# Two convolutions and a joint network on one core: a leading tile of 360 outputs, triple tiles of 214 and 334, and conv1's weight sums spread over PSUM and GpSimd

## The chip, the core and the metric

The kernel runs on one core of one Trainium2 chip. The metric is the device time of one execution in microseconds. Five engines work side by side, each through its own queue in order, and wait for one another on semaphores: TensorE (PE; its weight loads are listed as PEld), VectorE (DVE), ScalarE (ACT), GpSimd (POOL), and SyncE (SP), whose queue issues nearly all DMA transfers here.

## The reference

```python
B, T, D, K, U = 2, 4000, 512, 5, 8
xp = pad(x, 2)                                    # along time
h = gelu(sum_i xp[:, i:i+T] @ w1[i])[:, ::2]      # conv1, every second output: 2000
f = gelu(sum_i hp[:, i:i+T1] @ w2[i])[:, ::2]     # conv2 of padded h, again every second: 1000
fe = f @ w_f;  ge = g @ w_g
j  = tanh(fe[:, :, None, :] + ge[:, None, :, :])  # 2 x 1000 x 8 x 512
out = j @ w_o
```

Inputs, weights and the output are bfloat16.

## The kernel before

Channels lie on the 128 partitions in four blocks (`NK` = 4); time runs along the free dimension. conv1 of the first sequence is done in three tiles, conv1 of the second in two, conv2 in one a sequence.

**The leading tile** (`direct`, L691) is a plain convolution: the first 408 outputs (`2 * NA`, `NA` = 204), five taps by four output blocks `m` by four input blocks `k`, 80 matmuls of 408 columns that accumulate in PSUM banks 0 to 3. Its input `xr` comes in by two plain DMAs (128 rows of four time steps, then the rest), is turned by TensorE (`turn`, L489: 32 transposes, 16 of them 128 columns wide and 16 of the rest's 78) and copied out of PSUM to `xs` by ScalarE and VectorE. Eight warming matmuls of 512 columns on a cleared tile `zero` (L419, `warm_mm`, L480) come before.

**The triple tiles** (`Triple`, L562, and `Unit`, L607) use a fast form that makes three neighbouring outputs from nine products instead of fifteen. A tile of n columns gives 3 n outputs; for each output block `m` (a unit) it issues nine products of four matmuls: t2, tm, sm, t1, s1, t0, s0, ti, si, of n columns each. The two tiles of the first sequence are 266 columns each (`N3`), their six input phases are read by transposing DMAs into `xq[0]` and `xq[1]` (`load_xq`, phases in the order 4, 0, 2, 1, 3, 5). Before its products a tile needs differences and sums of its input phases in `row` (`Triple.step`: d2, d1, d0 are doubled copies on ScalarE, the others are differences or sums on VectorE), and the products need combinations of the weights: `w1_x[0..2]` for tm, t2, sm and `w1_t[0..2]` for s1, s0, t1. These are made once by `w1part` (L542), in four pieces of 128 columns: a piece has five VectorE operations of 512 elements with fp32 intermediate results in SBUF (t = w0 + w4, u = 4 w4 + w0, u = 2 w2 + u, v = t - w2, t + w2) and two copies on ScalarE; the first and the third piece also make the combinations of w1[1] and w1[3] for two pieces.

Then come conv2 in two triple tiles of 334 columns, the features, and the joint: 31 groups of seven products (`Seven`), a form that saves one of eight half-size products, with sums on GpSimd or VectorE, evicting copies on ScalarE or VectorE, and stores.

**The order** of each engine's queue is written out by hand as a string of two-character numbers (`ORDER`, L69): the operation's place in the program's text. `Plan.edges` (L148) derives which operation depends on which from the cells of SBUF and the PSUM banks that they touch, and `emit` (L211) puts a semaphore wait where the two are on different engines. Operations made with `flex` may run on one of two engines; the string that lists them decides. The durations written at the operations (`cost`, `wire`) do not enter the program. Since every queue is in order, an operation that waits holds up all that stands behind it on its engine.

**Loads.** SP issues `xr` in two parts, then w1[0] in halves, w1[4] in halves, w1[2], w1[1], w1[3], each held back until an earlier one has landed (`gate`), then xq[0], xq[1] and `xp[2]`, six phases each. GpSimd clears the few columns behind the data of xq[1] once its phases have landed (L678). xq[0] shares its place with xs[1], xq[1] with the end of `w2_sb`.

Of the kernel before, what the change touches and what calls it, by code (L numbers as in the profile page):

```python
# [7 lines left out]
ACT = mybir.ActivationFunctionType  # L8
ALU = mybir.AluOpType
# [54 lines left out]
class Op:  # L64
# [6 lines left out]
        "0Y0Z0a0b0c0d0e0f0g0i0k0l0n0q0y0z0_0-101112131415161718191A1B1C1D1E1F1G1H1p2L2l321I1J2v2S2T1r1s2w2n2N2o2O34352y2V2z2W"  # L71
        "3F3G3C3D392s3X2t3A3Y3Q3S3g3T403a3b3q4A3n3i3r3j3d4J423e4T4B434U3o473t4L4j4M4D3u484E4h4W4Q4k4R5U4X4u4r4x4s4o524z4p4_4v"
        "5e55565y535f586667595W5X5b5c6U5_6W5h6e6X5-6f6u6h6i6364695i6-726b6c6w6A736x707H7a7J7K7y7R7k7O7l7S7h7U7P757V7i7c867d7_"
        "7-767n8c8C897o8A8M87838N8J848e8K8f8E8F8v8_8w8m8n989990918j8P958k8Q9B8x8y9M9O8p9P8q9T9U969Z9a9c9C9o9x9d9W9z9X9qA5ACA2"
        "ABA4A99sAWAGAI9tArAsANAKB3B4BAAiAQAjATBBARAUBMAlAmBeBNAoApBfBtAyAzBGBhBiA-BTBUB0BDBHBEBJCABzBaBKBbBWBXCBBkBlCQCHB_CI"
        "CNBnC0COC1BqBoCKBrCLCuCcC6CdCRCfCvCgCTCjCkC7CxCyCUDODSDBDCDTC_DeDEC-DFCnCoD1DVD2DWDfDYDKDZDlDoDLDpDmDwE1E2D4E4E5D5Db"
        "DcDxDsDtENE7E8EOEKEDEEEiEAEjEBELEcEXEYEdF7ETEoFLEUF0EfElFMEgF1F8FXEmFDFOFfF3FBFPFgFsF4F_G4F-FRFiG5FZFjFSFUFVG1G2GNGG"
        "GHGTGUFoFpFuGAGWG7G8GZGXGJGKGOGaGnGoGcGqGrGhGfHCGwGxH0GdHEH3H1HVH4H9HWHAHbHhH6I4I5HKHNHcHLH7HOHjHpHqHeHYHZHfHRHSIAI7"
        "I8IKHyHzHsIhIbIBILHtIcIiIDJ4J5INIOIRIeISIEIkJKIrIsIfJAJBIlJLJDI_J7IuIvJXI-J8JdJaJbJYJEJgJeJRJNJhK0K1JnJoJSJqJwJOKGK6"
        "JrK3K4KHKbJxK7KVKWK9KcKAKYKZL0KeKfKlKmKNL1KOKJKuL6KKKoL7LZKpL3LTL9KvLGLULaLHLALcL4LyLNLsLjLOLkLtLzLdLJLKLWM2LXM3MCMR"  # L80
        "L-M0MSMuMDMvLmLnM5MJM6MhMiMKMFMUMXMGMVMYMaMxMyMbM_N1M-NPN8N9MoMkNQMpN2MlNBNCNFNGNSNTNYNuNvO1ONNZOONfNgNiNjNVNWN_O2Nx"
        "NyN-O8OdNmOeNnO9OwOTOWOUOxOqOrOXOBOQOCOtOROFOkOuOGP4OzP5OgPBPCOlOhP7O_PHPIPKP8PLPiQ9PjPQPRPNPOQAPXPYPaPrPoPpPbPsPlPm"
        "PyPePfPzQMP-Q0Q3Q4QNQCQDQIQJQFQGQPQQQTQUQXQYQbQeQfQi"),
    "act": (
        "080h0m1U0r1x1W1a1z1Z251Y2b1q271K2m1L2M1-1j2U1t2x1l1M1O332d2R1N3E2g2f2X2u2_3Z3B3H3R2h3h413c2r3K3s3M4K3x3f4C4V3p3y3w38"
        "494F4b3m3W3v4i5V5D464t4Y4P4S4y4d5C574q4w5z5B4n6E5A5g5154685d6V6g786j6v6G6M6a5j65795S6B5a745T627I7A7b6d7s5x7z7T717N6_"
        "7W7j7m5q6T7Q5w778D8d7u7g828O8B886s6t7p6S8X8-8L858o8Y9A8W9G8I8R8i8l9N7G948r9I976m9b9V9D9e9S8z9p9_9rA69YAcAXA8AFAtAdAP"
        "AfAMAeAhASAnBOAVB8BuB9AgBgCFCECs9wB7CGCqB-CJC2CCCrCDCeCwChDQCtDPDRFJDDD-CpE0DGDgEaDnFHCXEbE3D6FxFFFGFID_FwEMEFEZEPGS"
        "FyEpFNF2FYFKG_FCF5FhFzIWFkG-GIGVFvI0IVJ2GpGRGgGsHDJVH2J_HXI2IYHMHPI6I1IXIaJ-IMICIjJ6IdJ3ItI3IZJMIwJWJZK_JfK2JpKTJsNN"
        "KILSKdKRK-KnL2KUKyKqLwL8LVLILRLlL_NqKSLxM4MTMEMwMtMjMHKzMQNsN0MPMmNDNLNRMsOPNhNwNXNkNtNMOfOMNOODNrOpP6OLOiPJOoP9PPPZ"  # L90
        "PkQBPcPqP_Q1QOQHQRQgQdQk"),
    "dve": (
        "000j0o0p1R1S1v1T1V1X231w1u212Z1_1y24221b2a261d1c1Q1e1g1f1P1h1i1k28202p1m2P2Y362c1n2Q2q372e1o302i2k2j2-3U3I3V313J3L3k"
        "3P3z3l3O3N4H3-444I3_4N454Z4l4G4m4a4O4c4-4f4e504g5m5E5G5F5k5Y6D6J6F6C5l5Z5P6Y6l6L6K6Z605Q615N5O5t5p6I7C6H7D7Y6y7B5R5u"
        "6z7L7M7Z6P7q5o7X6Q5r7E6k5s5v7r7e6N806O7t7f6R816p7v6n7w6o6q7x6r8G7F8H8b8g8Z8h8u928t939H8a9F9h9f9Q9l9j9R9g8s9k9J9E9i9n"
        "9y9K9-A09mADA3A7AAA1AEAJ9uAHAOAL9vB5B69LAkAYAZBPAbAuBQAvBCAqA_BjBVBIBFBvB1BYBcBmBLByCaBpCMCPBsCZClC8CzCbCVDUCSD0CWD8"
        "DkDXEyEGEzEHD3DqDMDaE6DdDyDuEqDzEtErGCE9EkECEeEvFbEwEVEhEnFEF9FQExGjFtG6G0FTFaFWG3FqGBG9GYGLGbGPGiHHIGHlHIGyGeHFH5Hi"
        "HBHdH8HkHrHaHgHTI9H_HuIHIoJGIPIFITIgJHIpImJCJ9J0JcJFJjKDJkJiJPJTK5JyKXK8KBKaKgKPKLKjKkLDM8KwLbLfM9L5LBLPLuLYLLM1LeLo"
        "M7MAMBMdN4MLMZMWMzNAMqMcNHNUN3OZNdNbO4NcO5NaO3NzNoOAOVO0OsOSOyOvOHOmPDOYO-PMP2PTPuP3PUPvPSPnPgPtQ5QEQKQVQZQcQj"),
    "pool": (  # L100
        "01020304050s0t0u2A0v0w0x295n8VAaBSAwBRAxBwCYDjBxD9D7DhDiE-DAE_EJEsEIFcEuFeGkFdGlGDHGGFGEHmIIGmHoHJHnJIInIqIJJJKCJlKF"
        "KhKEJmLCKiLFLgLELiLhMfMeN5MgN6N7NeO6O7OaOcObP0P1PWPVPwPx"),
    "sp": (
        "0607090A0B0C0D0E0F0G0H0I0J0K0L0M0N0O0P0Q0R0S0T0U0V0W0X2B2C2D2E2F2G2H2I2J2K5H5I5J5K5L5M8S8T8UB2BZBdC3C4C5C9CiCmDHDIDJ"
        "DNDrDvEQERESEWF6FAFlFmFnFrGMGQGtGuGvGzHQHUHvHwHxH-IQIUIxIyIzJ1JQJUJtJuJvJzKMKQKrKsKtKxLMLQLpLqLrLvMIMMMNMOMnMrNENINJ"
        "NKNlNpOEOIOJOKOjOnPAPEPFPGPdPhQ2Q6Q7Q8QLQSQWQaQh"),
}


class Plan:  # L110


    COMPUTE = ("pe", "act", "dve", "pool")
    HOP = 0.16

    def __init__(self, nc):
        self.nc = nc
# [1118 lines left out]
```

## Time and profile before

| | |
|---|---|
| three runs, median | 248.95 us (248.75 to 248.99) |
| span of the profiled execution | 247.2 us |
| runs' median less that span | 1.75 us |
| PE busy | 242.8 us, 1932 matmuls |
| DVE busy | 224.8 us |
| ACT busy | 210.7 us |
| POOL busy | 83.8 us |
| granted clock of TensorE | full in all 40 slices |

The profiled execution's own time is its span, from its first instruction to its last; the times of the runs also hold what lies around it. Shares are of the span. In a row of a timeline the first number is the start, the second the length, then engine, line, operation, tiles (written <- read), shape and count; in brackets stands the idle time before it and what ended it. Most matmuls bear the line of one helper (L412), so groups are told apart by tiles and shapes. PEclk is the clock that the throttle granted; whether the array runs at full pace is read from the distance between matmuls.

### The profile page before, as it was taken

What the parts mean: (1) busy time and instruction counts of PE and PEld (TensorE: products, weight loads), DVE (VectorE), ACT (ScalarE), POOL (GpSimd) and SP (SyncE); (2) the same over time, 40 slices, a digit from 0 to 9 for tenths busy, and PEclk for the clock granted to TensorE, in tenths of its full rate; (3) what the DMA queues carried; (4) which work ended last, traced back from release to release, by engine and by line L of the source; (5) the groups of instructions that cost most, each with busy time, mean ns of one, the idle gap of its engine ahead of it and who ended that gap; (6) DMA issues with size and microseconds to landing.
All of it is one profiled execution on the core that took longest, in us unless ns stands there. A gap on an engine that the chain in (4) does not pass through costs nothing.

```text
span 247.2 us, 5277 instructions
## 1 busy us (share of the span) xinstructions
PE 242.8 (98%) x1932; PEld 186.1 (75%) x1932; DVE 224.8 (91%) x403; ACT 210.7 (85%) x359; POOL 83.8 (34%) x90
## 2 busy tenths in 40 slices
PE   8999999999999999999999999999999999999995
PEld 4657888877666666666567888778788888888883
DVE  1799998867999999699998999999999999999994
ACT  3269799899669857986799999999999999999992
POOL 1000000000000000000015584677887886796861
PEclk9999999999999999999999999999999999999999
DMA  6998999997700340000000234413433655356377
GB/s 215 331 193 168 185 157 205 150 177 174 254 2 3 119 135 3 1 1 3 0 0 3 85 102 139 143 48 129 131 127 103 195 171 172 132 187 200 123 258 233
DMA packets 57890, 31.87 MB, mean 129 GB/s; under 512 B 33835, under 2 KB 57659, under 8 KB 57865
## 3 DMA queue, kind: packets, MB, share of 16 engines
q1 hardware_dynamic: 57577, 31.41, 48.5%
q8 instruction: 15, 0.25, 0.4%
q10 hardware_dynamic: 288, 0.13, 0.2%
q14 instruction: 10, 0.08, 0.1%
HBM read 7.66 MB, written 16.38 MB: 97 GB/s over the span
## 4 chain that ended last, share of the span: by engine, by line
PE 98%; DVE 0%; issue 0%
PE acc L412 97%; PE acc L496 1%; DVE ost L835 0%; DVE xs L505 0%; DVE zero L419 0%
## 5 line engine op out<-in xcount | busy, mean ns | idle before, releaser
L398 DVE TENSOR_TENSOR og<-acc,sn 128x512 bf16<-128x512 f32 x93 | 60.0, 690 | 1.9 <-PE acc L412 1.2
L412 PE MATMUL acc<-tw,ss 128*128 128x256 f16 x372 | 58.0, 273 | 0.0
L404 ACT ACTIVATE jT<-feT,geT 128x1000 bf16<-128x1000 f32 (+6 forms) x56 | 53.2, 1002 | 1.8 <-DVE feT L398 1.5
L834 ACT ACTIVATE sn<-acc 128x512 f32<-128x512 f32 (+1 forms) x70 | 43.0, 707 | 1.0 <-PE acc L412 0.7
L412 PEld LDWEIGHTS acc<-tw,ss 128*128 128x128 f16 x372 | 36.0, 98 | 6.5 <-ACT sn L834 0.2
L903 POOL TENSOR_TENSOR ss<-jT 128x512 f16<-128x512 bf16 x24 | 27.7, 1168 | 25.0 <-DVE feT L398 22.5
L412 PE MATMUL acc<-row,w_sb 128*128 128x334 bf16 (+1 forms) x192 | 31.7, 296 | 0.0
L412 PE MATMUL acc<-wo_sb,jT 128*128 128x256 bf16 x176 | 29.2, 273 | 0.0
L404 ACT ACTIVATE sd<-acc 128x334 f32<-128x334 f32 (+1 forms) x48 | 20.6, 435 | 10.1 <-PE acc L412 9.6
L412 PE MATMUL acc<-row,w_x 128*128 128x266 bf16 (+1 forms) x192 | 28.4, 291 | 0.0
L404 ACT ACTIVATE jX<-feT,geT 128x1000 bf16<-128x1000 f32 (+4 forms) x28 | 27.4, 1042 | 0.0
L394 POOL MEMSET hT<- 128x8 bf16 (+2 forms) x6 | 0.7, 149 | 70.5 <-ACT hT L404 70.5
L412 PEld LDWEIGHTS acc<-row,w_sb 128*128 128x128 bf16 x192 | 18.7, 98 | 6.3
L412 PEld LDWEIGHTS acc<-row,w_x 128*128 128x128 bf16 x192 | 18.7, 98 | 5.7
L903 POOL TENSOR_TENSOR ss<-jT,ss 128x512 f16<-128x512 bf16 x14 | 16.6, 1189 | 15.1 <-DVE ss L903 9.7
L412 PE MATMUL acc<-wo_sb,ss 128*128 128x256 bf16 x124 | 21.0, 273 | 0.0
L412 PEld LDWEIGHTS acc<-wo_sb,jT 128*128 128x128 bf16 x176 | 17.2, 98 | 3.1
L835 DVE COPY sn<-acc 128x512 f32<-128x512 f32 (+1 forms) x25 | 16.8, 691 | 1.1 <-PE acc L412 1.0
L412 PE MATMUL acc<-hT,w_sb 128*128 128x334 bf16 x96 | 17.1, 305 | 0.0
L518 DVE SCALAR_TENSOR_TENSOR acc<-acc,sd 128x334 f32<-128x334 f32 (+1 forms) x24 | 11.7, 487 | 5.8 <-PE acc L412 5.6
L404 ACT ACTIVATE hT<-acc 128x266 bf16<-128x266 f32 (+2 forms) x36 | 14.6, 433 | 2.7 <-PE acc L412 2.4
L834 ACT ACTIVATE og<-acc 128x512 bf16<-128x512 f32 x22 | 15.3, 710 | 1.5 <-PE acc L412 1.5
(113 smaller groups left out, 502.5 us busy)
## 6 DMA issues: line engine op xcount, KB each, us to landing
out_dram<-og SPq DMA_DIRECT2D x45, 256.0 KB, 2.3
w_sb<-in_w_dram SPq DMA_DIRECT2D x8, 512.0 KB, 4.9
out_dram<-og SPq DMA_DIRECT2D x19, 128.0 KB, 2.2
w_sb<-in_w_dram SPq DMA_DIRECT2D x4, 256.0 KB, 4.8
xr<-in_x_dram SPq DMA_DIRECT2D x1, 512.0 KB, 3.5
wf_sb<-in_w_f_dram SPq DMA_DIRECT2D x1, 512.0 KB, 3.6
wg_sb<-in_w_g_dram SPq DMA_DIRECT2D x1, 512.0 KB, 5.1
wo_sb<-in_w_o_dram SPq DMA_DIRECT2D x1, 512.0 KB, 5.2
```

What stands on the lines that cost most here:

```text
L394: pl.op("pool", lambda e: e.memset(v.ap, 0.0), (), (v,))
L398: pl.op(eng, lambda e: e.tensor_tensor(out=o.ap, in0=a.ap, in1=b.ap, op=op), (a, b), (o,), 0.02 + 2.14e-3 * o.ap.free_size() if eng == "po ...
L404: pl.op("act", lambda e: e.activation(o.ap, i.ap, func, scale=scale, bias=0.0 if bias is None else bias.ap), rd, (o,), o.ap.free_size() * ...
L412: ins = e.matmul(o.ap, lhsT=l.ap, rhs=r.ap, start=start and n == 0, stop=stop and n == len(pairs) - 1, skip_group_check=not check)
L496: ins = e.transpose(pv.ap[:, i, k, :], xr[rt].h[0:n, 2 * r + pp, k, :], ident.h[0:n, 0:n])
L518: pl.op(eng, lambda e: e.scalar_tensor_tensor(out=o.ap, in0=a.ap, scalar=f, in1=b.ap, op0=ALU.mult, op1=add), (a, b), (o,), vec_cost(o, (a ...
L834: pl.flex({"act": (lambda e: e.activation(o.ap, v.ap, ACT.Copy), 0.05 + n * 0.833e-3), "dve": (lambda e: e.tensor_copy(out=o.ap, in_=v.ap) ...
L835: "dve": (lambda e: e.tensor_copy(out=o.ap, in_=v.ap), 0.065 + n * 1.04e-3)}, (v,), (o,))
L903: fn = lambda e, o=S[i], x=x, y=y, op=op: e.tensor_tensor(out=o.ap, in0=x.ap, in1=y.ap, op=op)
```

## The change

- **Tiles.** `NA` goes from 204 to 180, so the leading tile has 360 outputs, and the second part of `xr` has 54 rows for 78. The triple tiles of the first sequence go from (266, 266) to (214, 334). The loads of xq[0] become 224 rows a phase (272 before), those of xq[1] 336 (272 before). Both buffers get 352 columns; xq[0] then fills xs[1], and xq[1] reaches into w2[0].
- **Weight sums.** `w1part` now begins each piece with a ScalarE cast of w1[4] into a PSUM bank. In the first two pieces t, u and v live in PSUM and VectorE does their five sums. In the other two GpSimd makes t, v and t + w2 in SBUF, VectorE only the two steps of u. The combinations of w1[1] and w1[3] become operations of their own (`w13part`), two of which may go to VectorE or GpSimd.
- **Warming.** The tile `zero` is gone. The warming matmuls and the identity read constants that the preamble has made; the warming matmuls no longer depend on VectorE.
- **Scaled copies** (`scaled`) may go to ScalarE or VectorE: d0 to d2, next, prev and the units' copies c and s.
- **Loads.** w1[3] is gated on the first half of w1[4] and not on the second. The clearing of xq[1] is split by phase.
- **Orders.** All five strings are new. VectorE has 412 operations for 403, ScalarE 341 for 360, GpSimd 103 for 86; TensorE 722 and SP 140 as before. Among them: ScalarE's queue begins with the leading tile's copies, the casts of pieces 0 and 1, and then the copy of GpSimd's v of piece 2; GpSimd's has t, v, t + w2 of piece 2, t of piece 3, the difference of w1[1] and w1[3], v of piece 3, the clearing of xq[1]'s phases 4 and 0, and then t + w2 of piece 3; TensorE's has 76 of the leading tile's matmuls, t2 of units 0, 2, 1, the last four, t2 of unit 3, and the other products. The halves of the last tile are also stored in another order.

```diff
-    NA, N3 = 204, (266, 266)
+    NA, N3 = 180, (214, 334)
...
-        xq = [Buf(nc, f"xq{i}", [6, NK, (288, 288)[i]], BF16, v.end - v.bytes) for i, v in enumerate((xs[1], w2_sb))]
+        xq = [Buf(nc, f"xq{i}", [6, NK, (352, 352)[i]], BF16, v.end - v.bytes) for i, v in enumerate((xs[1], w2_sb))]
...
-        zv = zero[:]
-        pl.op("dve", lambda e: e.memset(zv.ap, 0.0), (), (zv,))
...
-            out=idv.ap, in_=zero[0:P].ap, compare_op=ALU.not_equal, fill=1.0, base=0,
-            pattern=[[-1, P]], channel_multiplier=1), (zero[0:P],), (idv,))
+            out=idv.ap, in_=nc.const_aps.tensor(0.0, [P, P], FP32), compare_op=ALU.not_equal, fill=1.0, base=0,
+            pattern=[[-1, P]], channel_multiplier=1), (), (idv,))
...
-                              (4, (slice(0, NK), slice(D // 2, D)), 0), (2, None, 1), (1, None, 3), (3, None, 5)):
+                              (4, (slice(0, NK), slice(D // 2, D)), 0), (2, None, 1)):
             load_w1(i, part, gate)
-        for ph in (4, 0, 2, 1, 3, 5):
-            load_xq(0, ph)
+        for kind, i in (('w', 1), ('w', 3), ('x', 4), ('x', 0), ('x', 2), ('x', 1), ('x', 3), ('x', 5)):
+            if kind == "w":
+                load_w1(i, None, len(came) - 4)
+            else:
+                load_xq(0, i)
...
         def warm_mm(n):
-            o, z, zz = ps.cols(3 * NT, NT), zero[0:P], zero[:]
+            o = ps.cols(3 * NT, NT)
+            one = [nc.const_aps.tensor(1.0, [P, k], BF16) for k in (P, NT)]
             for _ in range(n):
-                mm(o, [(z, zz)], True, True)
+                pl.op("pe", lambda e: e.matmul(o.ap, lhsT=one[0], rhs=one[1], start=True, stop=True), (), (o,))
...
+        WBANK = ((6, 7), (5, 4), (6, 7), (5, 4))
+        WHOME = ('P', 'P', 'G', 'G')
+
+        def scaled(o, i, f):
...
+            pl.flex({"act": (lambda e: e.activation(o.ap, i.ap, ACT.Copy, scale=f), n * 0.833e-3 + (0.05 if i.psum else 0.105)),
+                     "dve": (lambda e: e.tensor_scalar_mul(out=o.ap, in0=i.ap, scalar1=f), 0.065 + n * (0.26e-3 if fast else 1.04e-3))}, (i,), (o,))
...
         def w1part(m, part):
             sl = slice(m * P, (m + 1) * P)
             w = lambda i: w1_sb[i, :, sl]
-            if part == "s":
-                t, v, u = ssum[4][:], ssum[m % 2][:], ssum[2 + m % 2][:]
...
+            home = WHOME[m]
+            if home != "S":
+                u, t = (ps.cols(bk * NT, NT).map(lambda a: a.rearrange("p (k c) -> p k c", k=NK)) for bk in WBANK[m])
+                act(u, w(4), ACT.Copy)
+                w4 = u
...
+            if home == "G":
+                t, v = ssum[4][:], ssum[m % 2][:]
+                tt("pool", t, w(0), w(4), add)
+                tt("pool", v, t, w(2), sub)
+                tt("pool", w1_t[2, :, sl], t, w(2), add)
+            else:
+                v = t if home == "P" else ssum[m % 2][:]
+                tt("dve", t, w4, w(0), add)
+            stt("dve", u, w4, 4.0, w(0))
+            stt("dve", u, w(2), 2.0, u)
+            act(w1_x[1, :, sl], u, ACT.Copy, scale=1.0 / 3.0)
+            if home != "G":
+                tt("dve", w1_t[2, :, sl], t, w(2), add)
                 tt("dve", v, t, w(2), sub)
...
+            act(w1_x[0, :, sl], v, ACT.Copy, scale=1.0 / 3.0)
+
+        def w13part(m):
+            n = slice(m * P, (m + 2) * P)
+            shared(w1_x[2, :, n], w1_sb[1, :, n], w1_sb[3, :, n], sub, True)
+            shared(w1_t[0, :, n], w1_sb[1, :, n], w1_sb[3, :, n], add, True)
+            scaled(w1_t[1, :, n], w1_sb[1, :, n], 2.0)
...
-        memset(xq[1][0:4, :, 1 + N3[1]:4 + N3[1]])
-        memset(xq[1][4:6, :, N3[1]:4 + N3[1]])
+        for ph in (4, 0, 2, 1, 3, 5):
+            memset(xq[1][ph, :, (1 if ph < 4 else 0) + N3[1]:4 + N3[1]])
```

125 lines of the change are left out of this document (60 added, 65 removed).

## The prediction

> **What bounds the kernel now.** I read the page's head first, then the chain of work that ended last in order of time, then the waits of TensorE, then single stretches.
>
> ```profile
> span 247.2 us, 5277 instructions
> PE 98%; DVE 0%; issue 0%
> ```
>
> The chain in order of time (start, length, what) says what that 98% is:
>
> ```profile
> 0.86 0.28 DVE zero L419
> 1.14 0.05 issue
> 1.19 3.59 PE acc L412 x8
> 4.78 2.18 PE acc L496 x24
> 6.96 0.02 issue
> 6.99 0.33 DVE xs L505
> 7.32 0.05 issue
> 7.37 236.76 PE acc L412 x1892
> ```
>
> From 7.37 us to 244.13 us the chain never leaves TensorE. So a microsecond is won only by fewer matmul columns, by a stream that begins before 7.37, or after its end; and one is lost as soon as a matmul waits. The only wait of TensorE itself that the view of waits lists is the one for the cleared tile, at the start:
>
> ```profile
> PE acc L412 <- DVE zero L419: 1.2, 1, 1.2
> ```
>
> The other engines have little to give. The stretches below show busy time of PE, PEld, DVE, ACT and POOL, then clock, DMA share and GB/s. In 20 to 25 us VectorE and ScalarE are busy throughout, in 200 to 240 almost throughout:
>
> ```profile
> 20.00:25.00 5.00, 5.00 (x43) 3.90 (x41) 5.00 (x9) 5.00 (x11) 0.22 (x2) 1.00 0.94 180
> 200.00:240.00 40.00, 40.00 (x367) 35.37 (x366) 39.67 (x77) 39.99 (x67) 30.20 (x27) 1.00 0.55 177
> ```
>
> **Columns.** The timeline of TensorE gives the pace of a matmul by its width: the start of one group to the start of the next, over the count.
>
> ```profile
> 7.37 12.65 PE L412 MATMUL acc<-xs,w_sb 128*128 128x408 bf16 x72
> 19.86 1.98 PE L412 MATMUL acc<-row,w_x 128*128 128x266 bf16 x16
> 21.67 0.51 PE L412 MATMUL acc<-xs,w_sb 128*128 128x408 bf16 x2
> ...
> 62.37 1.86 PE L412 MATMUL acc<-xp,w_t 128*128 128x334 bf16 x12
> 64.07 0.30 PE L412 MATMUL acc<-row,w_sb 128*128 128x334 bf16 x1
> ```
>
> 408 columns: 12.49/72 = 0.1735 us. 266: 1.81/16 = 0.1131. 334: 1.70/12 = 0.1417. On the lines between these, 360 costs 0.1417 + 26/74 x 0.0318 = 0.1529 and 214 costs 0.1131 - 52/68 x 0.0286 = 0.0912. The leading tile has 5 taps x 4 x 4 = 80 matmuls: 80 x (0.1529 - 0.1735) = -1.65 us. A triple tile has 9 products x 4 x 4 = 144: 144 x (0.0912 - 0.1131) = -3.15 for the first, 144 x (0.1417 - 0.1131) = +4.12 for the second. Together **-0.68 us**; the triple tiles alone lose 0.97, since they now hold 548 columns for 532.
>
> **The start.** The warming matmuls wait for VectorE's memset of `zero`. Read from a preamble constant they wait for nothing, and can go when the engines are released:
>
> ```profile
> 0.31 0.10 POOL L1221 MEMSET const-bfloat16-1.0<- 128x1 bf16 x1
> 0.74 1.28 ACT L404 ACT_TABLE_LOAD   x1 [0.74 <-PEq L1221]
> 1.19 3.59 PE L412 MATMUL acc<-zero 128*128 128x512 bf16 x8 [1.19 <-DVE zero L419]
> 4.27 0.10 PEld L496 LDWEIGHTS acc<-ident,xr 128*128 128x128 bf16 x1 [0.40 <-DMA xr<-in_x_dram]
> 4.58 0.26 PEld L496 LDWEIGHTS acc<-ident,xr 128*128 128x128 bf16 x2 [0.20 <-issue]
> ```
>
> The constant lies there at 0.41, ScalarE goes at 0.74, so I put the first warming matmul at 0.78. The eight took 1.19 to 4.58 = 3.39, and now end at 4.17. What is late next is the load of `xr`, which let the first transpose's weights in at 4.27. So the transposes begin at 4.28, not 4.58. From there to 6.96 the chain had 16 transposes of 128 columns and 8 of 78:
>
> ```profile
> 4.58:6.28 1.70, 1.70 (x17) 1.70 (x16) 0.42 (x1) 0.60 (x1) 0.00 (x0) 1.00 1.04 306
> 6.28:6.74 0.46, 0.46 (x9) 1.00 1.16 336
> 6.75:7.06 0.31, 0.31 (x12) 1.00 1.20 299
> ```
>
> The first 16 take 1.70, or 0.83 ns a column; the 8 and the drain took the other 0.68. With 54 columns the 8 save 8 x 24 x 0.83 ns = 0.16. The evicting copy shrinks from 312 to 216 elements: between 0.33 (all fixed) and 0.23 (in proportion); I take 0.27. The stream begins at 4.28 + 2.22 + 0.03 + 0.27 + 0.05 = 6.85 instead of 7.37: **-0.52 us**. Bounds: nothing if the transposes are held by something else, about 1.2 if the clock comes early (third rival).
>
> **The clock.** Transposes of 78 columns came 0.066 us apart before 6.75 and half as far apart behind it: the array went to full pace 5.56 us after the first matmul. The Trainium skill (TensorE: Matmul & The Clock Gate, "Part 1: The HAM clock gate") puts that change about 4 us, give or take 0.5, into sustained matmuls, by a window that runs free of the kernel. The trace does not agree: 5.56. By that rule the change would come near 4.8 here, and the time would be that of the third rival.
>
> **Weight sums of conv1.** The stream reaches the first triple tile after 76 of 80 leading matmuls: 6.85 + 76 x 0.1529 = 18.47. One product of four matmuls then takes 0.365 us, so in the new order products are due at: t2 of unit 0 18.47, tm 20.54, sm of unit 0 21.27, t1 of unit 3 27.1. That is 1.4 us earlier than before (19.86) with VectorE already full, so its queue has to be added up. Prices:
>
> ```profile
> 7.99 0.69 DVE L398 TENSOR_TENSOR ssum<-w_sb 128x512 f32<-128x512 bf16 x1
> ...
> 10.77 0.69 DVE L518 SCALAR_TENSOR_TENSOR ssum<-w_sb,ssum 128x512 f32<-128x512 bf16 x1 [0.88 <-DMA w_sb<-in_w_dram]
> 11.38 0.69 DVE L398 TENSOR_TENSOR ssum<-ssum,w_sb 128x512 f32<-128x512 f32 x1
> 11.98 0.69 DVE L398 TENSOR_TENSOR w_t<-ssum,w_sb 128x512 bf16<-128x512 f32 x1
> ...
> 13.90 1.15 ACT L404 ACTIVATE w_x<-ssum 128x512 bf16<-128x512 f32 x2 [1.20 <-DVE ssum L518]
> ...
> L903 POOL TENSOR_TENSOR ss<-ss,jT x8: 1153/1159/1530, 138.4 to 233.1; 128x512 f16<-128x512 f16 x8
> L903 DVE TENSOR_TENSOR ss<-ss,jT x13: 417/421/653, 130.5 to 236.9; 128x512 f16<-128x512 f16 x13
> ```
>
> A sum on VectorE starts every 0.60 us and is done after 0.69; a copy on ScalarE takes 0.63; GpSimd's nearest operation of 512 elements takes 1.16 (min, median, max 1.15, 1.16, 1.53). A sum with PSUM operands is not in the trace at this shape: between 0.60 and, if PSUM costs a tenth of a microsecond more, 0.70. I take 0.60. ScalarE's cast of w1[4] into PSUM goes ahead of the first sum: 0.63 after the landing that let VectorE start at 7.99; the 96 KB less of `xr` bring that landing forward by about 0.3, so 8.4. In the new order fourteen sums precede the tile's first difference: 8.4 + 14 x 0.60 + 0.1 for a wait for ScalarE = 16.9, the difference of 856 elements 0.6, ready 17.5. Due 18.47: 1.0 to spare. Then d2, r1, r2, r0, tm at 0.3 to 0.52 each: tm 19.85 (due 20.54), sm 20.4 (due 21.27).
>
> GpSimd does t and v of the third piece first; ScalarE's third place in its queue is the copy of that v, and the casts and copies of the other pieces stand behind it. t can start when the second half of w1[4] is there, about half a microsecond behind the first, at 8.55, and ends at 9.7. v needs w1[2], which landed at 10.7 and now at about 10.4, and is done at 11.6. ScalarE's cast for VectorE's tenth sum, three operations behind that copy, is done at 13.9; VectorE arrives there at 13.8. So GpSimd may be late by about 0.7 us before TensorE waits.
>
> The thinnest place is t1 of unit 3. Its weights stand on GpSimd behind two memsets that need xq1's first two phases:
>
> ```profile
> 21.91 1.31 SPq L445 DMA_TRANSPOSE xq<-in_x_dram  x1
> ...
> L445 SPq DMA_TRANSPOSE xq<-in_x_dram x12: 1309/1618/2555, 9.2 to 28.1; - x12
> DMA to landing us min/median/max: 4.0/4.5/6.1
> ```
>
> The second phase, issued at 21.91, landed at about 26.4. At 1.62 us for 272 rows (5.95 ns a row) xq0 now has 6 x 48 rows fewer (-1.71), xq1 2 x 64 more (+0.76), `xr` gives 0.3: 25.15. The GpSimd sum is done at 26.3, due 27.1. With the max of 6.1 to land, 27.9: a wait of 0.8. GpSimd's 1.53 and VectorE's 0.65 above look like one engine holding up the other. The Trainium skill (SBUF — State Buffer, "Who interferes with whom") has a VectorE operation with two SBUF inputs and a GpSimd operation that reads SBUF shut each other out; those maxima agree. By it this sum could be held by one more VectorE operation, 0.69, which leaves 0.1 of the 0.8 to spare.
>
> I allow **+0.2 us** for such waits over the whole kernel: between 0 (all slacks as worked out) and 0.8 (this one lost), nearer the first.
>
> **What I cost at nothing.** Scaled copies that may go to VectorE, and joint sums shifted between VectorE and GpSimd (30 of VectorE's to GpSimd, 24 back): covered by the stream, 0.4 to 1.2 us each if it waits. Stores free of their old place, and the end's last evicting copy, which goes from VectorE to ScalarE: taken as equal. The wider xq1 now covers the end of w2[0], whose load waits for it; that load is used some 40 us later. xq1's first two phases are there at 25.2, and its first product is due at 29.7.
>
> **Sum.** -0.68 - 0.52 + 0.2 = -1.0 us. The span goes from 247.2 to 246.2. The three runs have a median of 248.95, 1.75 above the profiled span (launch and end); I keep that: **247.95 us**.
>
> **Rivals.**
> 1. Slower: GpSimd paces the sums. If its fp32 sums take 2.7 us, not 1.16 (no fp32 sum of GpSimd is in the trace), v of the third piece ends at 13.95, the ScalarE queue and VectorE follow 2.35 late, 0.7 is slack, 1.7 is wait. That is where it decides: -1.2 + 1.7 = +0.5. At 2.9 us each the wait is 2.05, and the time 248.95 - 1.2 + 2.05 = 249.8. Against: the eight of the row above never passed 1.53.
> 2. The start does not move: transposes still begin near 4.6, or the clock turns later by what was won. 248.95 - 0.68 + 0.2 = 248.45, no change that can be told. For: the clock depends on more than the first matmul. Against: the load's row at 4.27.
> 3. Faster still: the clock turns near 4.8. Five transposes slow, then eleven at 0.053 (half of 0.106), the 8 short ones likewise: the stream begins near 6.2, another 0.65: 247.3. It is what the Trainium skill's rule (TensorE: Matmul & The Clock Gate) would give.
>
> **Chances.** Forecast 0.50, first rival 0.18, second 0.17, third 0.15. A measurement tells about 0.2%, 0.5 us, from no change. The forecast and third case are faster: 0.65. The second lies at the bound and counts as the same, with a little of the rest: 0.17. Slower: 0.18. The range runs from the third rival less 0.2, 247.1, to the first, 249.8. The likeliest case's own range is 247.4 to 248.4.
>
> **What would show it.** Right: first matmul near 0.78, first leading matmul near 6.85, 80 of them at 0.153, products at 0.0912 and 0.1417, no idle PEld row over 0.2 us between 7 and 60. Wrong: PEld waits for `w_x` or `w_t` from POOL or ACT between 18 and 30; a chain through POOL; L518 or L398 longer than 0.69 beside GpSimd; the first leading matmul still behind 7.2; new PE waits after 200 us, where nothing was worked out.

## The result, and the profile after

The changed kernel takes 251.88 us (median, 251.07 to 252.33) against 248.87 us for the kernel before beside it: ratio 1.0116, 95% interval 1.0102 to 1.0130. It is slower, where 247.95 was forecast, and the time lies outside the range of 247.1 to 249.8. Medians here are over all runs; ratios leave disturbed runs out, so the two can differ by a tenth of a per cent or two.

The page's head of the kernel after:

```profile
span 250.5 us, 5275 instructions
PE 81%; DVE 8%; DMA 4%; ACT 3%; issue 2%; SPq 0%; ACTq 0%; DVEq 0%
```

98% of the chain was TensorE before; now VectorE and DMA hold 12% of it. Three places in the traces say where the time went. The middle one is the start of the 1001st of the 1932 matmuls: it lies in the joint in both kernels, and what comes before it is nearly the same work.

| | before | after | gained or lost on the way |
|---|---|---|---|
| stream of leading matmuls begins | 7.37 | 7.00 | -0.37 |
| 1001st matmul starts | 136.67 | 136.16 | -0.14 (in all -0.51) |
| last matmul starts | 243.84 | 246.22 | **+2.89** |
| end of the span | 247.16 | 250.51 | **+0.97** |

Half of the 0.51 is the order of the work alone: ahead of its 1001st matmul the kernel after has eight matmuls of 334 columns fewer and eight of 256 columns more, 8 x (0.1417 - 0.109) = 0.26 us. At equal work the lead, on which nearly all of the prediction was spent, gained 0.25 us, the joint layer, which was taken as equal, lost 2.63, and the end 0.97. The start, from TensorE's timeline (start, length, what):

```profile
0.78 3.57 PE L484 MATMUL acc<-const-bfloat16-1.0 128*128 128x512 bf16 x8 [0.78 <-PEq L1247]
4.28 2.68 PE L497 MATMUL acc<-ident,xr 128*128 128x128 bf16 x32
7.00 11.82 PE L411 MATMUL acc<-xs,w_sb 128*128 128x360 bf16 x76
18.65 1.28 PE L411 MATMUL acc<-row,w_x 128*128 128x214 bf16 x12
```

Warming at 0.78 and transposes at 4.28 are what was forecast, and the pace is too: (18.65 - 7.00)/76 = 0.1533 us for 360 columns. Then the joint and features, busy time of PE, PEld, DVE, ACT, POOL by stretch; before, then after:

```profile
160.00:243.80 83.80, 83.80 (x736) 70.97 (x735) 82.54 (x154) 81.72 (x135) 62.28 (x54) 1.00 0.49 158
```

```profile
160.00:246.20 86.20, 84.33 (x734) 70.36 (x732) 82.97 (x153) 80.19 (x129) 64.81 (x57) 1.00 0.47 150
```

With all but the same matmuls TensorE had no idle time before and 1.87 us now; VectorE is busy 0.4 us more, GpSimd 2.5 us more and ScalarE 1.5 us less, so no engine was handed much more work. From start to start of the matmuls the losses are 0.29 us at 172.9, 0.99 at 212.5, 1.07 at 227.0 and 0.18 at 243.3, together 2.53 of the 2.63. The waits of after (waiting <- waited for: us, times, longest), SyncE's issues from 205 us on, and then the chain around the two large ones (start, length, what):

```profile
DVE og L397 <- DMA out_dram<-og: 2.4, 2, 1.3
PE acc L411 <- DVE og L397: 1.7, 2, 0.9
```

```profile
205.13 0.56 SPq L882 DMA_DIRECT2D out_dram<-og  x1
205.74 1.12 SPq L984 DMA_DIRECT2D out_dram<-og  x2
206.90 1.56 SPq L882 DMA_DIRECT2D out_dram<-og  x3
```

```profile
207.91 0.04 SPq L882
207.94 0.04 issue
207.99 3.67 DMA out_dram<-og
...
211.78 0.70 DVE og L397
212.48 0.05 issue
212.53 0.84 PE acc L411 x6
...
222.25 3.85 DMA out_dram<-og
...
226.28 0.70 DVE og L397
226.99 0.05 issue
227.03 16.20 PE acc L411 x146
```

It reads forwards: SyncE issues a store late, at 207.99; it takes 3.67 us to land in a busy stretch (DMA share 0.78 from 210.0 to 212.5); only then is the output buffer `og` free (the ring has three), VectorE writes into it at 211.78, that frees a PSUM bank, and TensorE goes on at 212.53. The copies that fed that store were done at 205.10, 2.9 us before its issue: it stood in SyncE's in-order queue behind four stores whose data were ready between 205.10 and 205.70, and then behind one whose data came only at 207.57. Plainer still at 168.63, on the way to the first of the four gaps: a store ready since 162.00 goes then, behind one whose data came at 168.18. Measured from the end of the last copy to the issue, a store of the joint lies ready for 0.50 us on average before (3 of 94 over 2 us) and for 1.70 us after (26 over 2 us, the longest 10.2).

The end: what the DMA engines still have to move once the last matmul has started, before and then after:

```profile
DMA packets 1250, 0.66 MB, mean 196 GB/s; under 512 B 96, under 2 KB 1250, under 8 KB 1250
```

```profile
DMA packets 1564, 0.96 MB, mean 218 GB/s; under 512 B 113, under 2 KB 1564, under 8 KB 1564
```

### The profile page after: what moved, and what is told of

It reads as the page before. It is cut to its first block, busy times and chain, and to the rows that moved or that the text cites. A ratio compares the mean times of both kernels' runs of the same rounds, so it can differ in the third digit from the quotient of the medians.

```text
span 250.5 us, 5275 instructions
## 1 busy us (share of the span) xinstructions
PE 243.8 (97%) x1932; PEld 184.0 (73%) x1932; DVE 228.5 (91%) x412; ACT 195.7 (78%) x340; POOL 99.7 (40%) x107
## 4 chain that ended last, share of the span: by engine, by line
PE 81%; DVE 8%; DMA 4%; ACT 3%; issue 2%; SPq 0%; ACTq 0%; DVEq 0%
PE acc L411 78%; DVE og L397 4%; DMA out_dram<-og 4%; ACT sn L867 1%; PE acc L484 1%; ACT jX L403 1%; PE acc L497 1%; DVE ss L936 1%; DVE og L868 1%; DVE ft L586 1%; ACT og L867 1%; DVE sn L868 0%; SPq L984 0%; DVE sn L872 0%; ACTq L882 0%
## 5 line engine op out<-in xcount | busy, mean ns | idle before, releaser
L403 ACT ACTIVATE jT<-feT,geT 128x1000 bf16<-128x1000 f32 (+6 forms) x56 | 50.4, 951 | 0.2 <-DVE feT L397 0.2
L867 ACT ACTIVATE sn<-acc 128x512 f32<-128x512 f32 (+1 forms) x71 | 41.0, 619 | 5.6 <-PE acc L411 4.6
L936 POOL TENSOR_TENSOR ss<-jT 128x512 f16<-128x512 bf16 x22 | 25.6, 1172 | 29.8 <-ACT jT L403 26.4
L411 PE MATMUL acc<-row,w_x 128*128 128x334 bf16 (+1 forms) x192 | 29.5, 293 | 0.0
L548 ACT ACTIVATE sd<-acc 128x334 f32<-128x334 f32 (+1 forms) x38 | 15.9, 430 | 15.9 <-PE acc L411 15.6
L403 ACT ACTIVATE jX<-feT,geT 128x1000 bf16<-128x1000 f32 (+4 forms) x28 | 25.8, 943 | 0.0
L403 ACT ACTIVATE hT<-acc 128x334 bf16<-128x334 f32 (+2 forms) x36 | 15.0, 431 | 11.2 <-PE acc L411 10.7
L936 POOL TENSOR_TENSOR ss<-jT,ss 128x512 f16<-128x512 bf16 x15 | 18.1, 1206 | 10.9 <-DVE ss L936 6.9
L411 PE MATMUL acc<-xp,w_t 128*128 128x334 bf16 x96 | 16.2, 304 | 0.0
L411 PE MATMUL acc<-row,w_t 128*128 128x334 bf16 x96 | 16.2, 305 | 0.0
```

The costliest lines, as they stand in the source:

```text
L403: pl.op("act", lambda e: e.activation(o.ap, i.ap, func, scale=scale, bias=0.0 if bias is None else bias.ap), rd, (o,), o.ap.free_size() * ...
L411: ins = e.matmul(o.ap, lhsT=l.ap, rhs=r.ap, start=start and n == 0, stop=stop and n == len(pairs) - 1, skip_group_check=not check)
L548: pl.flex({"act": (lambda e: e.activation(o.ap, i.ap, ACT.Copy, scale=f), n * 0.833e-3 + (0.05 if i.psum else 0.105)), "dve": (lambda e: e ...
L867: pl.flex({"act": (lambda e: e.activation(o.ap, v.ap, ACT.Copy), 0.05 + n * 0.833e-3), "dve": (lambda e: e.tensor_copy(out=o.ap, in_=v.ap) ...
L936: fn = lambda e, o=S[i], x=x, y=y, op=op: e.tensor_tensor(out=o.ap, in0=x.ap, in1=y.ap, op=op)
```

## The experiments

Theory S: the stores' order, found anew, makes the loss behind 160 us, and the end is another small matter. Rivals: the compute orders of the joint are slow in themselves (J); the lead has a share. Numbers in the diffs of orders are operations' places in the program's text.

### The loss in the joint

**e1: program order for the stores.**

```diff
 ORDER["sp"], the 94 stores of the joint
-  as found anew (..., 973, 896, ..., 1309, 1313, 1280, 1342, 1279, ...)
+  in program order
```

> The changed kernel with one edit: SyncE's stores stand in program order again, as in the kernel before; all other queues stay. Theory S (stores that lie ready behind a later one return their og buffer late): the three waits of 0.29, 0.99 and 1.07 us before TensorE at 172.9, 212.5 and 227.0 go, so about 249.5 us (251.9 - 2.35), and stores issued over 2 us after their data fall from 26 of 94 to a handful. Rival J (the new division of the joint's work over VectorE, ScalarE and GpSimd is slower by itself): 251 us or more, with waits of TensorE on VectorE or GpSimd in other places.

255.58 us, ratio 1.0266 (1.0220 to 1.0313): 3.7 us slower still. S as stated fell. The new copies are not in program order either, so now SyncE waits for late data ahead of early ones; 24 stores lie over 2 us. On average they lie 1.32 us, less than in after, and the time is longer all the same: it counts which store lies, and who waits for its buffer. One stop of TensorE cost more than its length (timeline of PE; then busy time by stretch, the number behind POOL is the granted clock):

```profile
208.74 0.38 PE L411 MATMUL acc<-wo_sb,jT 128*128 128x256 bf16 x2
211.34 0.61 PE L411 MATMUL acc<-tw,ss 128*128 128x256 f16 x4 [2.22 <-DVE og L397]
...
212.67 1.06 PE L411 MATMUL acc<-wo_sb,jT 128*128 128x256 bf16 x4
213.52 1.06 PE L411 MATMUL acc<-tw,ss 128*128 128x256 f16 x4
```

```profile
208.00:211.30 3.30, 1.12 (x11) 0.75 (x8) 0.76 (x3) 3.30 (x6) 3.17 (x3) 1.00 0.71 231
211.30:213.50 2.20, 2.16 (x16) 1.79 (x17) 2.20 (x4) 1.20 (x3) 2.20 (x3) 0.80 0.65 210
213.50:216.00 2.50, 2.50 (x14) 1.79 (x12) 1.56 (x4) 0.00 (x0) 1.35 (x2) 0.50 0.04 13
```

The wait of 2.22 us is followed, 1.3 us after its end, by 3.41 us at half the clock: four matmuls take 0.85 us (212.67 to 213.52) where four took 0.44 (211.34 to 211.78).

**e5: the stores in the order in which their data were ready.** Only SyncE's string changes; the five compute orders stay. This is the test that tells the queue (Q) from the compute orders (J).

```diff
 ORDER["sp"], the 94 stores of the joint
-  as found anew
+  sorted by the end of the last copy into each store's source, in the trace of after
```

> The changed kernel with one thing altered: from the joint layer on, SyncE issues its 94 stores in the order in which their data were ready in the trace of the changed kernel; all five compute engines keep their orders. Theory Q (only the order of SyncE's queue makes the loss: a store that is ready lies behind one whose data come later, and the ring of three output buffers passes the delay on to VectorE and TensorE): TensorE's waits of 0.3, 1.0 and 1.1 us at 172.9, 212.5 and 227.0 shrink to under 0.3 in all, stores lie ready 0.5 us on average instead of 1.7, and the time is 249.3 to 249.8, what is left over the kernel before being the tail. Rival J (the orders of the compute engines in the joint layer are slow in themselves: the data of several stores become ready together, and a queue in any order delays some of them): waits of 1.5 us or more stay behind stores, and the time is 251.0 or more.

250.00 us, ratio 1.0070 (1.0040 to 1.0101): 1.9 us of the 3.0 are gone. Stores lie ready 0.41 us on average (1 over 2 us), the waits at 172.9, 212.5 and 227.0 are gone, and one of 0.18 us at 211 is left. (Two later traces with the same joint, e11 and e13, lose 0.87 and 0.53 us behind 200 us: 0.18 is a good draw.) The median is 0.2 above Q's range, far from J's 251.0. So most of the loss is the order of SyncE's queue. The chain:

```profile
PE 93%; DVE 4%; issue 1%; ACT 0%; ACTq 0%; DVEq 0%
```

The last matmul starts at 243.28, 0.56 ahead of before; and the end is 0.66 behind before, since the tail (last matmul's start to the end of the span) is 4.54 us for 3.32.

**e6 and e14: a fourth output buffer.** e6 adds it from the fifth group of seven products on under after's order of stores; e14 from the ninth on under the sorted order.

```diff
+        og.append(at("og3", [4, NT], BF16, sd[0].end - sd[0].bytes))
...
-                self.o = og[self.n % len(og)]
+                self.q = self.n % 3 if self.n < 8 else (3, 2, 0, 1)[self.n % 4]    # e14
+                self.o = og[self.q]
```

> The changed kernel with a fourth output buffer in the joint layer's ring (from the fifth unit on, in memory that is idle by then); all orders stay, that of the stores too. Theory R (the loss is late stores passed on by the ring of three): the evicting copies no longer wait for a store of three units before, TensorE's waits of 1.0 and 1.1 us at 212.5 and 227.0 fall under 0.2 each even though the stores lie as long as before, and the time is 249.3 to 249.8. Rival P (the stores are late because the copies before them are late, and PSUM or VectorE's own queue holds TensorE): the waits stay at over 1.5 us in all, ended by VectorE without a store ahead of it, and the time is 251.0 or more.

253.66 us, ratio 1.0208 (1.0184 to 1.0232), slower than after. It does not tell R from P, since the place of the buffer was a wait of its own: the copy into it stood until ScalarE had read the last of conv2's sums there, and TensorE lost 0.71 and 0.67 us at 155.3 and 157.8, where after lost nothing. VectorE's timeline:

```profile
152.72 0.68 DVE L398 TENSOR_TENSOR og<-acc,sn 128x512 bf16<-128x512 f32 x1
154.55 0.69 DVE L398 TENSOR_TENSOR og<-acc,sn 128x512 bf16<-128x512 f32 x1 [1.15 <-ACT fT L404]
```

Behind 200 us it still lost 2.4 us (1.29, 0.38, 0.25, 0.14, 0.31): with stores as late as these a fourth buffer was no cure there.

> The run with stores sorted by their readiness, with a fourth output buffer from the ninth unit on, in memory whose last reader is done by 155 us (in the first run with four buffers the copies into it waited for that reader). Theory R (what the sorted stores leave of TensorE's waits behind 200 us, 0.2 to 0.9 us in the runs that have this order there, is the landing time of stores passed on by the ring of three): no wait over 0.1 us behind 200 us, and 249.4 to 249.8. Rival: TensorE waits there for VectorE's queue itself, and the time is within 0.15 us of 250.0.

249.78 us, ratio 1.0024 (1.0002 to 1.0045). R is right in the trace: behind 200 us no wait over 0.1 us is left, and from the 1001st matmul to the last it loses 0.04 us against before at equal work. So the compute orders of the joint cost TensorE nothing in themselves ahead of the last matmul. Against e5 the median falls by 0.2, which is less than the runs' spread, against after by 2.1. This is the lowest median with all five compute orders of the change; what holds it over the kernel before is the tail, 4.51 us.

**e3 and e7: the lead of the one, the joint of the other.** The orders of after up to the 700th operation (e3) or the 840th (e7), and from there those of before on all queues; SyncE's stores stand as before throughout.

> The changed program with its new orders up to the first feature product (tiles, sums, warming, conv1, most of conv2), and the order of the kernel before, with its choice of engines, for everything behind. Theory S plus T: nothing of the late loss is left, the lead is 0.3 us ahead when 150 us of products are left, so about 248.5 us (248.87 - 0.3), between 248.2 and 248.9. Rival L (the new lead upsets the joint by its timing): 250 us or more.

> The changed kernel up to its 840th operation (to about 163 us), and from there the order of the kernel before on every engine, without the seam that the earlier hybrid had at 135 us. Theory (the loss sits in the new order behind 163 us; the lead and the fewer columns are a gain of 0.4 to 0.5 us there): 248.3 to 248.7, no wait of TensorE over 0.3 us behind 30 us, and a tail from the last matmul's start to the end of the span of 3.2 to 3.5. Rival (the new lead and the new columns have no gain of their own, and the hybrid's loss was not the seam): 249.2 to 249.8.

249.83 us, ratio 1.0036 (1.0020 to 1.0051), and 249.51 us, ratio 1.0025 (1.0009 to 1.0040). In both the late loss is gone (stores lie ready 0.50 us, as before) and the tail is back at 3.38 and 3.35. But both seams cost: in e3 TensorE loses 1.26 us at 135.67, waiting for ScalarE, in e7 0.37 at 149.9 and 0.22 at 166.2. With e7's lead losing 1.00 us in its trace (below), the theory's 248.3 to 248.7 was not reached; 249.51 lies in the rival's range, though the seam is a loss and the lead a gain, 0.19 us at equal work. A splice of two orders is not the sum of its parts.

### The tail

**e2: the last copy ahead of the store's issue.** In after ScalarE's last copy stood behind an issue of 1.27 us on its own queue.

```diff
 ORDER["act"], end
-  ..., 1717 (store of the other half), 1709 (last copy), 1710 (its store)
+  ..., 1709, 1717, 1710
```

> The changed kernel with one edit: at the end of ScalarE's queue the evicting copy of the last half stands ahead of the issue of the other half's store, not behind it. Theory T (the issue of 1.27 us holds the last copy from 246.5 to 247.4): about 251.0 us, 0.9 less, and the stretch from the last matmul's start to the end of the span falls from 4.3 to about 3.4 us. Rival: the end is set by SyncE's stores of the same time (landed 249.75 against 249.93), then at most 0.2 less.

251.74 us, ratio 1.0120 (1.0104 to 1.0136). The copy now starts 0.31 us after the last matmul's start, at 245.74, and the tail is 4.42 us all the same: the last copy was not what the end waits for.

**e10 and e15: finishing the last pair of blocks earlier.** Under the sorted stores a few operations behind 222 us (e10) or 230 us (e15, with e14's buffers) are moved by some places in the queues of all five engines.

> The run with stores sorted by their readiness, with operations behind 222 us moved by a few places in the queues of TensorE, ScalarE, VectorE and SyncE so that the last whole pair of blocks (256 KB) is finished and stored earlier. Theory B (the tail is the time that the DMA engines need for the bytes that are still to be stored when the last matmul starts, 0.94 MB against 0.66 MB in the kernel before, at about 300 GB/s): the bytes left fall, the tail falls from 4.5 us to 3.3 to 3.9, and the time is 249.2 to 249.6. Rival F (the tail is set by the last copy and the fixed time of one store): the tail stays over 4.2 us and the time within 0.2 us of 250.0.

> The run with sorted stores and four buffers, with a few operations behind 230 us moved so that fewer bytes are left when the last matmul starts. Theory B (bytes left set the tail; the waits that ate the gain in the first attempt came from the ring of three): under 0.8 MB left, a tail under 4.0 us, waits behind 200 us under 0.3 us in all, and 248.9 to 249.4. Rival N (an order that stores earlier makes TensorE wait for it: bytes and matmuls can't both come earlier with these copies): the tail falls, waits of over 0.5 us appear behind 230 us, and the time is 249.6 or more.

252.18 us, ratio 1.0135 (1.0120 to 1.0151), and 250.40 us, ratio 1.0058 (1.0034 to 1.0082). In e10 the tail fell as theory B says:

```profile
DMA packets 1176, 0.58 MB, mean 169 GB/s; under 512 B 96, under 2 KB 1176, under 8 KB 1176
```

and the time did not: from 212 us on TensorE lost 3.6 us in ten waits for copies and stores, 0.71 the longest. e15 is rival N in small: 0.53 and 0.21 us lost at 233 and 0.22 at 243.7, more than the tail won. All traces together, bytes left at the last matmul's start against the tail:

| MB left | tail, us |
|---|---|
| 0.58 (e10) | 3.33 |
| 0.66 (before, e3, e4, e7, e8, e9, e12) | 3.30 to 3.38 |
| 0.85 (e15) | 3.91 |
| 0.93 to 0.95 (e2, e5, e6, e11, e13, e14) | 4.33 to 4.54 |
| 0.96 (after) | 4.30 |
| 1.23 (e1) | 5.41 |

Above 0.66 MB that is 3.0 to 4.4 us a megabyte, near the 0.26 MB a microsecond that after moved from 246.22 to its last landing at 249.93; in e10, the only trace below, the tail does not shrink further. The tail goes with the bytes in all traces, and the two edits that moved the bytes moved it; that the last matmuls and the bytes can both come early with these copies was not shown.

### The lead

**e4: the warming alone.** The kernel before, warming from the constant.

```diff
-                mm(o, [(z, zz)], True, True)
+                pl.op("pe", lambda e: e.matmul(o.ap, lhsT=one[0], rhs=one[1], start=True, stop=True), (), (o,))
```

> The kernel before with one edit: the warming matmuls read the preamble constant, the cleared tile stays for the identity. The start theory of the prediction: first matmul near 0.78, transposes from 4.28 instead of 4.58, 0.3 us less: 248.55 us. If the clock turns earlier with the first matmul as well, about 0.5 us more: 248.0. If the transposes or the clock are held by something else: 248.87, no change.

248.84 us, ratio 1.0006 (0.9994 to 1.0018): nothing that the medians show. The stream begins at 6.59, 0.78 earlier in its trace, and TensorE gives 0.34 of it back at 23.4 and 28.1; 0.42 is left at the end of the span, but that trace is of the fastest of ten runs. The chain up to there no longer holds a matmul of the leading tile:

```profile
5.66 4.72 DMA w_sb<-in_w_dram
...
21.39 1.97 DVE row L398 x3
23.36 0.05 issue
23.41 220.33 PE acc L412 x1788
```

A load, VectorE's weight sums behind it and its row differences set 23.41, whatever TensorE does before.

**e9 and e12: the tile sizes alone, and with the warming,** under the orders of before.

```diff
-    NA, N3 = 204, (266, 266)
+    NA, N3 = 180, (214, 334)
-        xq = [Buf(nc, f"xq{i}", [6, NK, (288, 288)[i]], ...
+        xq = [Buf(nc, f"xq{i}", [6, NK, (352, 352)[i]], ...
```

> The kernel before with the tile sizes alone changed: a leading tile of 360 outputs and triple tiles of 214 and 334, every order, the warming and the weight sums as before. Theory C (the columns are worth what the rows of before give for them, 0.68 us, and the order of the joint layer that went with them made the loss): 248.1 to 248.4, stores that lie ready no longer than before and a tail of 3.2 to 3.5 us. Rival L (TensorE only comes earlier to the same landings of the second input tile and to VectorE's sums): 248.7 to 249.0, with new waits of TensorE between 19 and 30 us of 0.5 us or more in all.

> The kernel before with the new tile sizes and with warming from the constant, orders and sums as before. Theory G (both gains are real and add up where the joint layer's order is the old one): 0.2 to 0.4 us less than the tile sizes alone, 247.8 to 248.2. Rival L (whatever makes TensorE earlier in the lead is given back at the next landing, as with the warming alone): within 0.1 us of the run with the tile sizes alone.

253.18 us, ratio 1.0190 (1.0145 to 1.0234), and 252.79 us, ratio 1.0143 (1.0111 to 1.0176); single runs lie between 250.69 and 255.47. Both theories fell, and the rival in size. The joint is as before (stores lie ready 0.51 us, tails 3.31 and 3.30), so all of the loss is in the lead: 5.2 us of waits up to 36 us in e9's trace, 3.1 in e12's, and in e9's another 1.6 at half the clock behind them. Of e9's six runs the three with a mean clock of 0.993 take 254.2 to 255.5, the others 252.1, so a part of its loss is the clock's. e9's chain and, after a wait of 2.76 us, its clock:

```profile
28.53 5.98 DMA xq<-in_x_dram
34.51 0.05 issue
34.56 0.14 POOL xq L394
34.70 0.02 issue
34.72 0.87 DVE row L398
35.59 0.05 issue
35.63 214.58 PE acc L412 x1692
```

```profile
32.00:36.00 4.00, 1.24 (x13) 0.91 (x11) 2.10 (x3) 3.94 (x8) 0.19 (x2) 1.00 1.25 165
36.00:40.00 4.00, 4.00 (x22) 2.63 (x21) 3.60 (x7) 2.45 (x4) 0.00 (x0) 0.61 1.07 196
```

The narrower tile is over sooner and the wide second one loads longer. Only together with the change's new lead orders, split sums and split clearing do these tile sizes come without that loss; which of the three it takes was not tested.

**e8: two waits of the lead moved.**

```diff
 ORDER["pe"]   -  149, 171 (sm of units 0, 1), 192 (tm of unit 2)    +  192, 149, 171
 ORDER["act"]  -  140 (the "prev" copy), 172                +  172, 140
```

> The run before this one, with two operations of the lead moved: TensorE's matmuls on unit 0's weight sums go behind the first product of unit 2, and ScalarE's copy of the previous columns, which waits for the last part of the second input tile, goes behind an eviction that does not. Theory A (the two operations stand in their queues ahead of work that is ready, and cost 0.2 to 0.5 us): 0.2 to 0.4 us less than the run before this one, 248.0 to 248.3. Rival L (the lead is bound by the landings of the loads and by VectorE's sums, and TensorE only waits elsewhere): within 0.1 us of the run before this one, the waits turning up at the next product.

250.15 us, ratio 1.0058 (1.0045 to 1.0071), 0.6 above e7: worse than either said. VectorE has an operation that needs copy 140 (141) ahead of a weight sum for TensorE (127). Later, 127 ran into GpSimd's last weight sum, took 1.64 us, and TensorE waited 1.16.

**e11 and e13: earlier landings, and no last GpSimd sum.** e11 is e5 with three quarters of w1[3] cleared, not loaded, so a part of conv1's sums is left out; e13 leaves out GpSimd's sum for the fourth block as well.

```diff
-                load_w1(i, None, len(came) - 4)
+                load_w1(i, (slice(0, 1), slice(0, D)) if i == 3 else None, len(came) - 4)
...
-                tt("pool", w1_t[2, :, sl], t, w(2), add)
+                memset of it where m == 3                                   # e13 only
```

> The run with stores sorted by their readiness, with three quarters of the tap w1[3] not loaded but cleared by GpSimd, so that part of conv1's sums is left out and the outputs are not the reference's; every matmul, copy and store is still issued. Theory L (the lead is bound by the landings of the loads: a start that is earlier by 0.5 us and fewer columns only bring TensorE sooner to the first triple's tile): the second input tile lands 1.0 to 1.5 us earlier, TensorE's waits between 19 and 27 us fall under 0.15 us in all, and the time is 249.4 to 249.7. Rival V (VectorE's and ScalarE's queues set the lead): landings earlier, the waits as before, and the time within 0.1 us of 250.0.

> The run with less weight loaded, with GpSimd's last weight sum (1.16 us, of the fourth block of columns) replaced by clearing its result, so that this sum is left out too. Theory K (earlier landings only let that sum run beside VectorE's row operation, which then takes 1.35 instead of 0.60 us and holds TensorE for 0.50 us at 26.35): the row operation takes 0.6 us, the wait at 26 us is under 0.1 us, and the time is 249.5 to 249.8. Rival (another operation of VectorE is stretched or is as late): a wait of 0.3 us or more between 24 and 28 us, and the time within 0.1 us of 250.1.

e11: 250.11 us, ratio 1.0061 (1.0045 to 1.0077), e5's time; e13: 249.99 us, ratio 1.0038 (1.0018 to 1.0058). In e11's trace the third to sixth phases of the first input tile land 0.8 to 1.1 us earlier than in e5's, VectorE's row differences come no earlier (their own queue holds them), and TensorE loses 1.02 us in the lead for e5's 0.18. One row each of VectorE, GpSimd and TensorE of e11:

```profile
24.94 1.35 DVE L397 TENSOR_TENSOR row<-row 128x856 bf16<-128x856 bf16 x1
24.67 1.16 POOL L397 TENSOR_TENSOR w_t<-ssum,w_sb 128x512 bf16<-128x512 f32 x1
26.35 1.09 PE L411 MATMUL acc<-row,w_sb 128*128 128x214 bf16 x10 [0.33 <-DVE row L397]
```

and of VectorE and TensorE of e13:

```profile
24.95 0.59 DVE L397 TENSOR_TENSOR row<-row 128x856 bf16<-128x856 bf16 x1
25.86 1.26 PE L411 MATMUL acc<-row,w_sb 128*128 128x214 bf16 x12
```

With GpSimd's sum away the row operation takes 0.59 and TensorE goes 0.49 us earlier: the mechanism of theory K. The price was not confirmed: the median fell by 0.12, not by 0.3 to 0.6; e13's trace has a wait of 0.53 us at 212.4, in the joint, where nothing was altered.

In the traces with the change's lead there are thus three outcomes:

| | row difference of VectorE that needs xq[0]'s fifth phase starts | GpSimd's last weight sum | 1001st matmul, before 136.67 |
|---|---|---|---|
| after, e1, e2, e10 | 20.74 to 20.96, held by the landing | out of the way | 136.00 to 136.21 |
| e7, e11 | 20.30, 20.39 | starts 0.3 us ahead of the row operation, which takes 1.31, 1.35 | 136.15, 136.22 |
| e5, e6, e13, e14, e15 | 20.07 to 20.31 | starts behind it, or is left out (e13) | 135.51 to 135.76 |

(e3 and e8 are left out of the table: the one has its seam, the other its moved waits ahead of that matmul.) The third row is 0.91 to 1.16 ahead of before, 0.65 to 0.90 at equal work; the forecast was 1.0. In the first the tile's fifth phase lands at 20.71 to 20.94, where e5, e6, e14 and e15 have 19.80 to 20.18. In after:

```profile
20.87 0.60 DVE L397 TENSOR_TENSOR row<-xq 128x856 bf16<-128x856 bf16 x1 [0.30 <-DMA xq<-in_x_dram]
```

No run beat the kernel before.

## Why the prediction was wrong

**Columns, -0.68: held** as far as it can be seen. 360 columns cost 0.1533 for 0.1529; the 214-column matmuls of e13's rows above come at 0.091 (8 of them from 25.13 to 25.86) for 0.0912. But e9 shows that the sum says nothing by itself: under old orders the same columns came with a median 4.3 us higher.

**The start, -0.52: the mechanism right, the size 0.37 in after's trace.** First matmul 0.78 and first transposes 4.28 come to the hundredth; the second is luck, for over the other traces with this warming it is 4.13 to 4.80. The stream began at 7.00, not 6.85. The second part of `xr` was not what was late, for nothing is waited for ahead of its first weights:

```profile
6.09 0.75 PEld L497 LDWEIGHTS acc<-ident,xr 54*128 54x128 bf16 x16 [0.20 <-issue]
```

Its first transpose comes 0.25 us after the last of the first part, where before has 0.11; why is open. Over all traces with the early warming the stream began between 6.42 and 7.23, and a part of that is the clock. By the traces' record of the granted clock the array is at full clock from 6.75 on in before, as the prediction read it off the transposes, and from 6.78 in after, 6.00 us after its first matmul for 5.56. So the second condition of rival 2, a clock that turns later by what was won, did come in after's trace, though the transposes moved. In the other fourteen, with the first matmul at 0.77 or 0.78 in each, the full clock came anywhere from 3.82 to 6.66. Ten of the fifteen have it by 5.35, where rival 3 wanted it near 4.8, and began their stream at 6.42 to 6.80; its 6.2 (its own terms add up to 6.0) came in none. The 5.56 us of one trace was one draw, and was taken as fixed. That the start's worth is what TensorE wins there was the other mistake: e4's trace won 0.78 and kept 0.42, and its median did not move.

**Weight sums and the allowance of +0.2: too small.** GpSimd's sums took 1.16 us, as the nearest row had it, so rival 1 (2.7 us each) fell, and TensorE waited for GpSimd nowhere in after. But after's tile difference waited for a landing, and the lead and columns together gave 0.25 at equal work, where -0.68 - 0.52 + 0.2 = -1.0 was forecast: the start gave 0.37, and there are 0.39 us of small waits up to 26 us and 0.25 in two stops at 113.9 and 117.5; about 0.2 is not accounted for. The best of eleven traces gives 0.90, so the sum was a best case and not a middle. The place called thinnest, GpSimd's sum behind two landings, was the right place; what goes wrong there was told as that sum being late, and what happens in e7 and e11 is that it is early and VectorE is held. The Trainium skill (SBUF — State Buffer, "Who interferes with whom") says that of two such operations the one that issues first has the port and the other stands for its whole length. The traces agree: GpSimd first, and VectorE's 0.60 becomes 1.31 and 1.35; VectorE first by 0.05 us (e14), and GpSimd's 1.16 becomes 1.56.

**"Stores free of their old place, and the end's last evicting copy ... taken as equal": this step failed,** and it carries 3.6 of the 4.3 us by which the span misses its forecast; the lead carries the rest. The first half cost 2.63 us from the 1001st matmul to the last; e5 takes back 1.9 us of the time, and e14 2.1, by SyncE's order and a buffer alone. The second half cost 0.97 us, and not by the copy that was named (e2) but by 0.30 MB more that was still to be stored. The change's rows were there to be read: 94 stores in a new order on one in-order queue, behind a ring of three, with the DMA share at 0.55 from 200 to 240 us. What was priced were operations; what cost the time is who stands behind them. The prediction's last line, "new PE waits after 200 us, where nothing was worked out", names the place, with no chance given to it. The scaled copies and the joint sums that changed engines, "covered by the stream", held: with the stores sorted and a fourth buffer (e14) the joint loses 0.04 us.

What stays open: whether any order has both the change's early matmuls and before's 0.66 MB at the end; the two tries did not. And which of several unsettled landings made after's own first tile late is not shown.

## What to carry to other kernels

When all orders are new, price the queues first: for every store or load on an in-order queue, ask whether its data come before those of the entries ahead of it, what buffer it frees, and who writes there next. A start that is won is worth only what the next landing lets through, so look for the chain up to the last wait of the lead before counting it. And count the bytes still to be stored when the last matmul starts; here each 0.1 MB over 0.66 cost 0.3 to 0.4 us.

## What the runs showed of the hardware that was not expected

- **The clock fell after short waits.** Waits of 2.22 us (e1) and 2.76 us (e9) were followed, 1.3 and 1.2 us after their ends, by 3.41 us at a granted clock of 0.50 (212.64 to 216.05, 36.86 to 40.27); after waits of up to 1.31 us (e1, at 238.16) it stayed full. The Trainium skill (TensorE: Matmul & The Clock Gate, "Part 1: The HAM clock gate") puts the fall behind an idle window of about 3.4 us; the two waits here were shorter, so the measurement goes ahead of that figure.
- **The full clock comes at a time that moves from trace to trace.** With the same warming and the first matmul at 0.77 or 0.78 us in fifteen traces, it came at 3.82 to 6.78.
- **An issue can take four times as long.** ScalarE's issue of a 64 KB store took 1.27 us at 246.11 in after, with SyncE issuing one store after another at the time, and 0.34 us at 247.84; in seven traces with SyncE so occupied (after, e5, e6, e11, e13, e14, e15) it took 0.93 to 1.40. An issue is work on the issuing engine's own queue.
- **Stores' landing times nearly double in busy stretches:** of after's two 64 KB stores the one at 205.13 took 2.08 us and the one on the chain, at 207.99, 3.67; the other on the chain, of 8 KB, took 3.85. The DMA shares at their ends were 0.78 (210.0 to 212.5) and 0.88 (225.5 to 227.0); the median of the 256 KB stores is 2.5.
